# A fused attention and gated-MLP kernel on one core: the written order of its pieces and their engines, written anew

## The chip, the cores and the metric

The kernel runs on one core of a Trainium2 chip. The metric is the device time of one execution in microseconds, the median of several. A core has five engines with instruction streams of their own: TensorE (PE in the profile, with its weight loads as PEld), VectorE (DVE), ScalarE (ACT), GpSimd (POOL) and SyncE (SP), which here issues nearly all DMAs. Each executes its stream in order and waits on semaphores for the others.

## The reference

```python
def _attn_ref(q, k, v):                      # (8, 8, 576, 64) each
    factor, Sd = 4, S // 4
    scale = 1.0 / np.sqrt(D)
    q_d, k_d, v_d = (mean over groups of 4 positions of q, k, v)
    out_d = softmax(scale * q_d @ k_d.T) @ v_d          # 144 x 144, whole
    out_up = np.repeat(out_d, factor, axis=2)
    mask = np.abs(pos[:, None] - pos[None, :]) < factor  # a band of 7
    out_local = softmax(where(mask, scale * q @ k.T, -1e9)) @ v
    return out_up + out_local

def _moe_ref(x, w_in, g_ln, w_sg, b_sg, w_out):          # x: (8, 576, 512)
    h = gelu_tanh(x @ w_in)                              # 1024 wide
    u, v = h[..., :512], h[..., 512:]
    v_n = (v - mean(v)) / np.sqrt(var(v) + 1e-06) * g_ln
    v_s = np.einsum('ts,bsd->btd', w_sg, v_n) + b_sg[None, :, None]
    return x + (u * v_s) @ w_out
```

The attention's output, with its heads side by side, is the `x` of the second function.

## The kernel before

The work is cut into 2105 named pieces (`Task`), each a few instructions of one engine. The program does not run them in loops: a string, `ORDER`, lists all pieces, and the program emits them in that order, so each engine's stream is the string with the other engines' pieces taken out. A word is a name, and after a slash the engine where there is a choice (V VectorE, A ScalarE, P GpSimd, S the SP queue). `place` also reads the string: it gives every piece that takes a buffer the one that was freed longest ago, out of 8 PSUM banks (`ps`), 10 buffers of kind `X` and 38 of kind `R` (`SIZES`). So the order also sets which earlier reader a piece has to wait for.

There are 8 batches, each with 4 pairs of heads, hence 32 pairs `g`. Names of a pair carry `g`; names of the second part carry the batch and an index.

- Loads on SP: `lq`, `lk`, `lv`, `lw` (q, k and two forms of v; 293, 293, 448 and 320 KB), `w…` (weights, 512 KB each; `wq0` to `wq4`, 288 KB), `small` (constants and the band mask, 463 KB) and `b`.
- Weights: `wq`, `wu`, `wb`, `wt`, `wh`, `wl` turn each weight into a high and a low part, once, on ScalarE, VectorE and Pool.
- Attention of a pair: `qs`, `ks`, `vs` sum groups of four. TensorE makes scores, `S` (local, line 424) and `Y` (pooled, line 445) for the first four pairs and both in one piece `YS` afterwards. Then come mask (`ma`, `mb`, line 432), maxima (`mx`, `my`), biases (`nx`, `ny`, lines 461 to 475), exponentials on ScalarE (`ea`, `eb`, line 484; `ec`, line 492), sums (`re`, `rc`), normalisation (`np`, `nq`, lines 506 and 509), transposes on TensorE (`T`, `U`, `t`, lines 512 and 521), their copies out of PSUM (`pa`, `pb`, `pc`, `pe`, line 221), and the product with v on TensorE (`D`, lines 573 and 589). `oe`, `od`, `xa`, `xb` join both results to `x` (line 596), `xh` and `xl` split it in a high and a low part (lines 221, 608), `xc` copies a rest.
- Second part of a batch: on TensorE `v` (line 691; in batch 0 split by its inner index into `vk` pieces and `v0.…`), `u` and `s` and `o` (all line 769; 12, 14 and 12 matmuls of 288 columns; in the last batch four `o` are split into `ok` and a rest). Between them `vg`, `vb`, `vp`, `vn`, `vh`, `vl` (activation, statistics, root, normalisation at line 740, split), `ua` (gelu, line 788), `sa` (line 807), `sm` (the gate, line 814), `gh`, `gl` (split, line 826), `oa` (line 843) and the store `os` (line 848).

TensorE's matmuls fall in three families: the big pieces `v`, `u`, `s`, `o` on the whole array; `S`, `Y`, `YS` and `D` on quarters of it (64 rows by 64 columns, 48 by 64); and the transposes. The batches overlap freely: attention pieces of the next batch stand between big pieces of this one.

Of the kernel before, what the change touches and what calls it, by code (L numbers as in the profile page):

```python
# [103 lines left out]
vp0.4 vn0.3 ua0.6 ua0.4 whq4/A xb4 vh0.2/A vl0.2/V vn0.4 U5 pa5/A pb5/A ua0.2 ua0.3 u0.5 vl0.1/V vh0.3/A vh0.4/A xh4/A
u0.7 vl0.3/V wur2 whr3/A wlr3/P t5 vl0.4/V wlq4/V s0.0 sa0.0 vs5 sm0.0/V s0.2 lq7 sa0.2 s0.1 eb6 wbr2 pc5/A pe5/A
xl4/V ea6 sa0.1 ua0.1 whr1/A s0.4 re6/V rc6 np6/V s0.3 s0.6 lw5 wtr2 whr0/A sm0.2/P sa0.4 lk8 whr2/A sm0.1/P gh0.0/A
sa0.3 sm0.3/V sm0.4/P qs7/V sa0.6 qs8/V ks8/V gl0.0/V s0.5 nq6/P lw6 ua0.5 gh0.1/A gl0.1/P ua0.7 sa0.5 sm0.5/V xc4
s0.7 sm0.6/P T6 D5 YS7 lq9 lv6 gh0.2/A sa0.7 sm0.7/V gl0.2/V wlr1/P my7 pa6/A lw7 oe5/V od5 ma7 gh0.3/A mb7 mx7 U6 xa5
gl0.3/P o0.6 vs6 oa0.6 lk9 wlr0/V xb5 ny7/A ec7 t6 pb6/A pc6/A pe6/A nx7/A ea7 o0.7 qs9/V D6 oe6/V od6 lv7 oa0.7 os0.3
vs7 YS8 lk10 lq10 wlr2/P eb7 ma8 mb8 mx8 nx8/V ea8 my8 re7/V xa6 rc7 np7/V o0.4 oa0.4 o0.5 oa0.5 ny8/A o0.1 nq7/P T7  # L110
U7 xh5/V eb8 xl5/V xc5 ec8 t7 ks9/V o0.3 pa7/V pb7/V pc7/V o0.0 pe7/V D7 re8/V rc8 xb6 oa0.0 oa0.1 oe7/V lv8 od7 xa7
YS9 lq11 ma9 lk11 nq8/P np8/P T8 U8 xh6/A xl6/P xb7 my9 xh7/A mb9 mx9 ny9/A t8 ec9 pa8/A pb8/V pc8/A xl7/P pe8/V xc7
nx9/A v1.1 vg1.1 vb1.1 vs8 v1.0 vg1.0 qs10/V lw8 D8 lv9 xc6 ks10/V oe8/V od8 ks11/P v1.4 va1.4/V ea9 eb9 re9/A vb1.0
v1.3 xa8 vg1.3 vj1.4 vg1.4 vp1.1 vn1.1 rc9 np9/V v1.2 vg1.2 T9 vs9 nq9/V U9 xb8 vp1.0 vn1.0 vh1.0/A pa9/A vl1.0/P
vb1.3 vh1.1/V pb9/A YS10 my10 ny10/A lq12 ma10 mb10 ec10 mx10 lw9 nx10/A pc9/A t9 pe9/V o0.2 oa0.2 vb1.2 u1.4 D9 oa0.3
qs11/P YS11 vp1.3 vb1.4 lk13 eb10 vn1.3 vh1.3/V lw11 os0.0 ea10 vp1.2 vn1.2 vp1.4 ma11 mb11 lv10 mx11 my11 ny11/V u1.2
re10/A rc10 oe9/A od9 xa9 u1.3 lq13 vl1.3/P vh1.2/A vl1.2/P u1.0 ua1.0 u1.1 np10/P T10 vn1.4 vh1.4/V ua1.4 nq10/P t10
ua1.2 vl1.4/P ua1.1 vs10 U10 pa10/A pb10/A vl1.1/V s1.1 pc10/V sa1.1 s1.0 ec11 nx11/A pe10/A xb9 lw10 D10 eb11 oe10/A
lk12 ks12/V qs12/V sa1.0 ks13/V lv11 YS12 my12 ma12 s1.2 ea11 re11/A rc11 sm1.1/P nq11/V ny12/A ec12 mb12 s1.4 vs11
mx12 nx12/V eb12 ea12 od10 ua1.3 s1.3 re12/A u1.6 lk14 os0.2 qs13/V xa10 xb10 sm1.0/V sa1.2 sm1.2/P gh1.0/A u1.5 xh9/V  # L120
lq14 np11/V U11 ua1.6 sa1.3 sm1.3/V t11 T11 pa11/A gh1.1/V s1.5 rc12 nq12/V pb11/V xh8/A pc11/A qs14/P t12 xl9/V
np12/V sa1.5 sa1.4 pe11/A D11 YS13 ua1.5 oe11/A od11 xa11 xb11 lv12 vs12 T12 ma13 lk15 mb13 mx13 nx13/A eb13 u1.7
xh10/V s1.6 my13 sm1.4/V gl1.0/P ua1.7 xl8/V xc9 ny13/V sm1.5/V ea13 pa12/A ec13 re13/A s1.7 xh11/V xl11/P xl10/V v2.3
vg2.3 v2.0 vg2.0 sa1.6 sm1.6/P sa1.7 sm1.7/V gh1.2/V gl1.2/P v2.1 gh1.3/V gl1.3/P gl1.1/P o1.4 vg2.1 U12 pb12/A rc13
np13/V T13 oa1.4 nq13/P U13 pc12/A pe12/A xc11 lw12 ks14/V D12 YS14 lv13 lq15 qs15/V vb2.1 xc8 pa13/A pb13/A pc13/V
vs13 my14 ma14 mb14 ny14/A ec14 t13 pe13/V oe12/V od12 xc10 v2.4 va2.4/A ks15/P o1.5 mx14 u2.6 nx14/V ea14 eb14 o1.2
vp2.1 vn2.1 oa1.5 ua2.6 o1.0 vb2.0 vp2.0 vj2.4 vn2.0 vh2.0/V vl2.0/V vb2.3 xa12 xb12 oa1.0 lw13 lq16 qs16/V D13 YS15
ma15 lv14 oa1.2 my15 mb15 o1.6 oa1.6 vg2.4 vb2.4 oe13/V vs14 mx15 od13 vh2.1/A nx15/V lw15 o1.7 re14/V rc14 xa13 lk16
ks16/P v2.2 ny15/A vp2.4 vn2.4 o1.1 ec15 vg2.2 vb2.2 oa1.1 os1.0 u2.0 np14/P T14 pa14/A nq14/V t14 vp2.3 U14 vl2.1/V
pb14/A o1.3 vh2.4/A vp2.2 vn2.2 pc14/A vh2.2/V lw14 ua2.0 pe14/V xb13 eb15 vn2.3 vh2.3/V D14 lv15 oa1.7 YS16 ma16  # L130
oa1.3 vl2.2/V u2.4 ea15 mb16 u2.3 my16 ny16/V ec16 oe14/A vl2.4/P u2.5 xh13/V lq18 lq17 re15/A rc15 xh12/V od14 qs17/V
u2.1 vs15 xa14 mx16 nx16/V ua2.4 ua2.5 np15/V nq15/V vl2.3/P s2.1 eb16 s2.0 sa2.0 xb14 u2.2 xh14/V xl14/V sa2.1 ua2.1
u2.7 ea16 re16/A ua2.2 ua2.3 lw16 lk17 xl12/V qs18/V sm2.1/V rc16 np16/V sm2.0/V s2.2 gh2.0/A s2.3 sa2.3 U15 T16 t15
# [855 lines left out]
```

## Time and profile before

| what | value |
|---|---|
| timed executions | 586.85, 587.50, 587.54 us; median 587.5 |
| profiled execution, span from first to last instruction | 585.7 us |
| TensorE busy | 559.7 us, 96% |
| VectorE, ScalarE, Pool busy | 432.7, 354.0, 306.2 us |
| DMA | 63.21 MB, mean 108 GB/s |

The timed median lies 1.8 us above the profiled span. Busy time of TensorE counts modelled ends of pipelined matmuls, so a full row does not say that it could not be faster; the distance between the starts of two pieces is the better measure of what a piece costs.

### The profile page before, as it was taken

Reading aid. Unit: us, or ns where it says so; the run is one execution under the profiler, and the core shown is the slowest. Engines: PE = TensorE matmul, PEld = TensorE weight load, DVE = VectorE, ACT = ScalarE, POOL = GpSimd, SP = SyncE. Lnnn points to the kernel's source line nnn. Section 1 sums busy time; section 2 is a strip of 40 time slices with the busy share of each in tenths; the row PEclk is TensorE's granted clock in tenths of the full one; section 3 lists DMA queues with packets and bytes.
Section 4 is the critical chain, followed back from the end, with each engine's and each line's share of the span. In section 5 each row is a group of like instructions: output and inputs, shape, how many; then the busy total and the mean of one; then the engine's idle time right before and its main releaser. Section 6 shows DMA issues by size and latency. Waiting matters only on the chain.

```text
span 585.7 us, 17441 instructions
## 1 busy us (share of the span) xinstructions
PE 559.7 (96%) x6992; PEld 522.2 (89%) x6992; DVE 432.7 (74%) x947; ACT 354.0 (60%) x1227; POOL 306.2 (52%) x384
## 2 busy tenths in 40 slices
PE   4778999999999999999999999999999999999997
...
GB/s 318 305 281 286 14 48 128 158 118 137 144 26 98 97 83 58 96 157 63 16 134 193 13 194 90 59 134 42 37 62 230 118 100 1 113 1 1 41 2 121
DMA packets 30610, 63.21 MB, mean 108 GB/s; under 512 B 3520, under 2 KB 3776, under 8 KB 30528
## 3 DMA queue, kind: packets, MB, share of 16 engines
...
q10 hardware_dynamic: 576, 1.23, 0.6%
...
## 4 chain that ended last, share of the span: by engine, by line
PE 81%; DVE 8%; ACT 5%; issue 3%; DMA 1%; POOL 0%; SPq 0%; ACTq 0%; DVEq 0%; POOLq 0%
PE ps L769 49%; PE ps L691 15%; PE ps L573 4%; ACT X L484 3%; PE ps L512 3%; PE ps L589 3%; PE ps L424 2%; PE ps L445 2%; PE ps L521 2%; DMA small_sb<-in_small_dram 1%; ACT pd L492 1%; DVE R L740 1%; DVE wsg_l L352 1%; DVE st L721 1%; ACT L492 1%
## 5 line engine op out<-in xcount | busy, mean ns | idle before, releaser
L769 PE MATMUL ps<-wsg_h,R 128*128 128x288 f32 x576 | 120.8, 297 | 0.0
L769 PE MATMUL ps<-R,weight_r 128*128 128x288 f32 x768 | 109.4, 297 | 0.3 <-ACT pd L492 0.3
L769 PE MATMUL ps<-X,weight_z 128*128 128x288 f32 x512 | 108.2, 296 | 0.3 <-DVE X L432 0.3
L769 PEld LDWEIGHTS ps<-R,weight_r 128*128 128x128 f32 x768 | 103.8, 188 | 2.1 <-DVE R L826 0.4
L691 PE MATMUL ps<-weight_y,X 128*128 128x512 f32 x320 | 98.0, 400 | 0.1
L484 ACT ACTIVATE X<-X,nb 128x64 f32<-128x64 f32 x280 | 93.5, 338 | 3.2 <-DVE nb L463 2.8
L769 PEld LDWEIGHTS ps<-wsg_h,R 128*128 128x128 f32 x576 | 94.2, 188 | 0.2
L769 PE MATMUL ps<-wsg_l,R 128*128 128x288 f32 x320 | 92.8, 296 | 0.4 <-DVE wsg_l L352 0.4
L769 PEld LDWEIGHTS ps<-X,weight_z 128*128 128x128 f32 x512 | 83.9, 188 | 1.2 <-ACT weight_z L221 0.7
L769 PE MATMUL ps<-R,weight_z 128*128 128x288 f32 x256 | 75.4, 295 | 0.0
L691 PEld LDWEIGHTS ps<-weight_y,X 128*128 128x128 f32 x320 | 58.2, 189 | 12.5 <-POOL X L221 0.4
L769 PEld LDWEIGHTS ps<-wsg_l,R 128*128 128x128 f32 x320 | 60.2, 188 | 0.6 <-DVE wsg_l L352 0.6
L732 POOL TENSOR_TENSOR rs<-rs,nhalf 128x1 f32<-128x1 f32 (+1 forms) x40 | 24.5, 614 | 63.0 <-DVE rs L723 62.9
L807 DVE SCALAR_TENSOR_TENSOR vs<-ps,small_sb,b_sb 128x288 f32<-128x288 f32 x64 | 32.4, 513 | 32.6 <-PE ps L769 31.6
L484 ACT ACTIVATION_READ_ACCUMULATOR X<-X,nb 128x1 f32 x280 | 53.1, 190 | 0.0
L691 PE MATMUL ps<-weight_y,R 128*128 128x512 f32 x128 | 50.7, 396 | 0.0
L408 POOL TENSOR_TENSOR pairs<-R 112x256 f32<-112x256 f32 x56 | 44.6, 796 | 10.2 <-DMA R<-in_v_dram 10.2
L788 ACT ACTIVATE R<-ps 128x288 f32<-128x288 f32 x64 | 24.7, 411 | 40.9 <-PE ps L769 40.8
L221 ACT CAST R<-R 128x512 fp32r<-128x512 f32 (+2 forms) x44 | 28.0, 641 | 34.0 <-DVE R L814 14.2
L769 PEld LDWEIGHTS ps<-R,weight_z 128*128 128x128 f32 x256 | 48.1, 188 | 0.3
L826 POOL TENSOR_TENSOR R<-R,R 128x576 fp32r<-128x576 f32 x21 | 31.1, 1484 | 28.6 <-PE ps L521 14.4
L814 POOL TENSOR_TENSOR R<-R,vs 128x288 f32<-128x288 f32 x23 | 20.4, 894 | 45.2 <-DVE vs L807 39.2
(111 smaller groups left out, 1210.7 us busy)
## 6 DMA issues: line engine op xcount, KB each, us to landing
...
```

Of the source, the lines that this page charges most:

```text
L221: (nc.scalar.copy if e == "A" else ENG[e].tensor_copy)(**kw)
L408: ENG[e].tensor_tensor(out=pairs, in0=v[:, 0:2], in1=v[:, 2:4], op=ALU.add)
L484: nc.scalar.activation(out=st["ms"][:, t, :], in_=src, func=AF.Exp, bias=st["nb"][:, t:t + 1], scale=scale, accum_out=sums[par][:, t:t + 1])
L512: nc.tensor.matmul(out=out, lhsT=st["ms"][0:LD, 2 * c:2 * c + 2, :], rhs=turn_l, is_transpose=True, start=True, stop=True)
L573: nc.tensor.matmul(out=out, lhsT=lhsT, rhs=pdt[ks, probs, h * QC:(h + 1) * QC], start=first, stop=last)
L691: nc.tensor.matmul(out=acc, lhsT=r32(l), rhs=r32(weights[f"y{k}"][:, 0, w]), start=(i == 0 and ks[0] == 0), stop=(i == len(ops) - 1 and ks ...
L732: nc.gpsimd.tensor_tensor(out=rs[0:n], in0=rs[0:n], in1=nhalf[0:n], op=ALU.pow)
L769: nc.tensor.matmul(out=acc[:, 0:HALF], lhsT=r32(l), rhs=r32(r), start=(first and n == 0), stop=(last and n == len(ops) - 1))
L788: nc.scalar.activation(out=us[i // 2][:, half(i)], in_=at["ps", "m", b, "u", i][:, 0:HALF], func=AF.Gelu_apprx_tanh)
L807: nc.vector.scalar_tensor_tensor(out=vsb[i], in0=at["ps", "m", b, "s", i][:, 0:HALF], scalar=g_sb[:, i // 2:i // 2 + 1], in1=b_sb[:, half( ...
L814: ENG[e].tensor_tensor(out=u[:, half(i)], in0=u[:, half(i)], in1=vsb[i], op=ALU.mult)
L826: ENG[e].tensor_tensor(out=r32(gl[d]), in0=us[d], in1=gh[d], op=ALU.subtract)
```

## The change

The string `ORDER` is replaced by another order of the same 2105 pieces, with other choices of engine for some. No function, buffer count or instruction shape changes. The new string was sought by a planner with rules in which VectorE and Pool exclude each other and TensorE pays for changes between kinds of pieces; the planner is not part of the kernel. Of the choices, the gate `sm` is on Pool 30 times instead of 23 (of 64), `np` and `nq` 39 instead of 34 (of 64), `vh` on VectorE 20 instead of 15 (of 40). Both strings up to `v0.1`, and their ends:

```diff
-wy0 lk0/A lq0/A lq1/A small ks0/P wqy0/A wuy0 wby0 wty0 wy3 qs0/V S0 mx0 lw1/A qs1/P nx0/V ea0 why0/V wqy3/V Y0 my0
-lk1/S ks1/P wy1 wuy3 wby3 wqy1/V ny0/A ec0 wly0/P wby1 wty3 wuy1 wty1 wy2 wqy2/A S1 wuy2 wby2 Y1 my1 wty2 lq3 wz2 eb0
-mx1 re0/A rc0 ny1/A ec1 nx1/A ea1 nq0/P lk3 np0/P lk2 wuz2 S3 lq2 S2 wz3 wqz2/V wbz2 mx3 qs3/V lq4 mx2 eb1 wqz3/A T0
-pa0/V why3/V U0 t0 pb0/A lv0/S lw0/S nx2/A pc0/V pe0/V ks2/P qs2/P Y2 my2 re1/A rc1 ks3/P ny2/V D0 ea2 eb2 wbz3 qs4/V
-wz1 np1/P oe0/V ec2 re2/A nq1/P lk4 ks4/P lv1/S wtz2 od0 xa0 xb0 T1 pa1/A t1 U1 pb1/V pc1/V pe1/A nx3/A Y3 my3 ea3 rc2
-np2/P nq2/P wqz1/A ny3/A YS4 xh0/V ma4 mb4 my4 mx4 eb3 ec3 wz0 D1 xl0/P lv2 wbz1 nx4/V T2 lw2 lq5 U2 re3/V oe1/A
-wly3/P rc3 np3/P lk5 whz2/A wlz2/P t2 pa2/A wqz0/A pb2/V pc2/V wq3 vk3.0 pe2/A qs5/V ny4/A ec4 D2 wr0 od1 xa1 wuz0
-nq3/P wbz0 eb4 T3 vk1.0 lv4 lv3 oe2/V od2 ks5/P xa2 xb2 xb1 lw3 pa3/A wq1 lk6 t3 U3 pb3/V pc3/V wr3 xh1/V why1/A
-wly1/V YS5 pe3/A D3 ma5 my5 ea4 re4/A rc4 nq4/V wuz3 lw4 t4 oe3/V wtz0 xl1/P vk3.1 why2/A wly2/P mb5 wr1 xh2/A xl2/V
-ks6/V ny5/A mx5 ec5 b lq6 od3 xa3 xb3 xh3/V np4/P xc0 wqr0/A lv5 wur0 wtz3 vk0.0 vk0.1 wq2 xc2 wqr1/A xl3/V nx5/A
-qs6/V vk0.2 vk2.0 vk2.1 wbr0 vk2.2 vk4.0 wqr3/A wur3 ea5 eb5 vs4 wbr1 wuz1 vk1.1 vk1.2 v0.1 lk7 re5/A wtr0 T4 pa4/A
...
-vh7.3/A vl7.3/V vl7.2/P oa6.1 os6.0 ua7.3 s7.0 s7.1 sa7.1 sa7.0 sm7.0/V ua7.5 sm7.1/P s7.2 sa7.2 sm7.2/P s7.4 sa7.4
-sm7.4/P ua7.6 ua7.7 s7.3 sa7.3 s7.5 gh7.0/V sm7.3/V gh7.1/V sa7.5 sm7.5/V gl7.1/P gh7.2/V s7.7 s7.6 o6.6 gl7.2/P
-gl7.0/V ok0 ok2 sa7.7 sm7.7/V ok1 sa7.6 sm7.6/P gh7.3/V gl7.3/P o7.0 oa7.0 o7.4 oa7.4 o7.5 oa7.5 oa6.6 o7.1 oa7.1 o7.2
-oa7.2 ok3 oa6.7 os7.2 os6.3 o7.6 oa7.6 os7.0 o7.3 os6.2 oa7.3 os7.1 o7.7 os7.3.0 oa7.7 os7.3.1
+lq0/A lk0/S ks0/V qs0/P Y0 my0 ny0/A small ec0 wy3 wuy3 wqy3/V wby3 wty3 wy1 wuy1 wqy1/V lq1/S qs1/P S0 mx0 lk1/S
+ks1/V nx0/A ea0 eb0 wby1 S1 mx1 Y1 my1 nx1/V re0/A ea1 lq2 why3/V ny1/V ec1 lk2 qs2/P S2 lw0/S ks2/P rc0 np0/V T0 wq0
+nq0/P U0 lq4 mx2 nx2/A wly3/V pa0/V pb0/V pc0/V lv0/S t0 eb1 pe0/A whq0/V wty1 why1/V wly1/P lk3 ks3/V lq3 S3 re1/A
+ea2 Y2 qs4/P wy2 lk4 rc1 D0 my2 ny2/A ec2 np1/P wy0 mx3 nx3/A wqy0/A oe0/V od0 xa0 xb0 wqy2/V xh0/V xl0/P T1 pa1/V wz2
+qs3/V ks4/P wby0 wq3 whq3/V wuy0 eb2 re2/A rc2 wby2 YS4 ma4 nq1/P U1 pb1/V wz1 wqz1/A xc0 wz3 wqz2/A ea3 mb4 my4 Y3
+my3 ny4/V wuy2 eb3 wq4 lq5 qs5/V pc1/V mx4 lv1/S lk5 ny3/A t1 pe1/A wlq0/P np2/P T2 pa2/A ec3 re3/A wbz2 wuz3 rc3 wbz1
+nq2/P U2 wty0 t2 wty2 pb2/A wuz1 wuz2 pc2/A pe2/V ks5/V ec4 lw1/S D1 oe1/V np3/P YS5 T3 od1 xa1 wqz3/A why0/A nx4/V
+xb1 wly0/V vk3.0 wtz2 nq3/P U3 xh1/V xl1/P lv2 whq4/A lw2 wtz1 ea4 pa3/A vk2.0 ma5 eb4 lv3 my5 ny5/A re4/A mb5 wbz3
+lk6 ks6/P pb3/A pc3/A wlq4/V rc4 np4/P D2 oe2/V od2 xa2 wr1 wqr1/A vk0.0 t3 lq6 ec5 wr2 why2/A wqr2/A wtz3 pe3/A mx5
+nx5/A lw6 xb2 xh2/A vk3.1 whz1/A vk2.1 vk0.1 wbr1 lw3 whz2/A wz0 wqz0/A wuz0 wr0 vk4.0 T4 pa4/V xc1 wly2/P vk1.0 wbr2
+vk4.1 vk1.1 D3 xl2/P xc2 vk4.2 vk2.2 vk1.2 whz3/A wbz0 oe3/A nq4/P U4 eb5 ea5 vk0.2 od3 xa3 xb3 vk3.2 wlz3/V wq1
+whq1/A xh3/V t4 wtz0 lk12 xl3/V xc3 v0.1 pb4/A wlq3/V lq7 wlz1/V qs7/V qs6/V wlz2/P vg0.1 vb0.1 lv4 vs4 re5/V v0.2
...
+u7.7 o6.2 oa6.2 vl7.0/V u7.1 u7.6 vl7.2/V vp7.3 vn7.3 vh7.3/V ua7.6 ua7.7 ua7.0 ua7.1 u7.2 u7.4 ua7.4 ua7.2 vn7.4
+vl7.3/V vh7.4/V vl7.4/V s7.1 sa7.1 s7.5 sm7.1/V s7.0 s7.2 s7.3 sa7.0 sm7.0/P sa7.2 gh7.0/V ua7.3 sa7.3 sm7.3/V sa7.5
+ua7.5 sm7.2/P gh7.1/A s7.4 sa7.4 sm7.4/P gl7.1/V gl7.0/P sm7.5/V gh7.2/V o6.5 s7.6 s7.7 gl7.2/V ok3 ok2 ok1 sa7.7
+sm7.7/P oa6.3 os6.1 ok0 sa7.6 oa6.5 sm7.6/P gh7.3/V gl7.3/V o7.4 o7.5 os3.0 o7.1 oa7.4 oa7.5 os6.2 o7.3 os5.0 os6.0
+o7.0 oa7.0 os7.2 oa7.1 os7.0 o7.2 oa7.2 oa7.3 os7.1 o7.6 oa7.6 os7.3.0 o7.7 oa7.7 os7.3.1
```

More of the change, by code (lines that the diff above doesn't have):

```diff
@@ L104 @@
[L104 to L133, printed above, removed]
@@ L144 @@
-os1.3 sa3.0 sm3.1/V sm3.0/P gh3.0/A xl17/P re18/A rc18 np18/V lq21 qs21/V s3.2 s3.3 ua3.4 u3.5 ua3.5 ua3.3 s3.4 s3.5
-oa2.5 sa3.2 sm3.2/V np19/P lw19 sa3.4 sm3.4/V sa3.3 sm3.3/V nq18/P gl3.0/P gh3.1/V U19 sa3.5 lw18 t18 T18 pa18/A xc16
-ua3.7 xc17 gl3.1/P U18 pb18/A sm3.5/V gh3.2/A pc18/V T19 pa19/A pb19/V pc19/V s3.6 s3.7 sa3.6 pe19/V pe18/A D18 lv19
-vs19 sa3.7 sm3.7/V YS20 ma20 mb20 oe18/A od18 xa18 D19 gl3.2/P sm3.6/P gh3.3/A oe19/A gl3.3/P o3.7 my20 lv20 xb18
-ny20/V ec20 o3.4 mx20 xh18/V lq22 od19 xa19 xb19 xh19/V nx20/A eb20 YS21 my21 ma21 lk23 mb21 mx21 oa3.4 nx21/V lq23
@@ L184 @@
-sm6.4/P ua6.5 sm6.5/V s6.7 gl6.1/V s6.6 sa6.6 sa6.7 sm6.7/V D30 lv31 vs31 pe31/A gh6.2/A gl6.2/V os4.0 oe30/A D31
-sm6.6/P gh6.3/A gl6.3/V o6.3 od30 xa30 o6.0 o6.1 xc28 xb30 xh30/V oe31/V o6.2 oa6.2 o6.5 o6.4 od31 xa31 xb31 xl30/P
-xh31/V xl31/V xc31 oa6.4 xc29 xc30 v7.4 oa6.0 va7.4/V u7.6 u7.2 ua7.2 vj7.4 v7.1 u7.0 ua7.0 v7.2 vg7.1 vb7.1 vp7.1
-vg7.2 vb7.2 vp7.2 v7.0 vg7.0 vb7.0 v7.3 vg7.3 vn7.1 vh7.1/V vn7.2 vp7.0 vn7.0 vb7.3 vg7.4 u7.7 vb7.4 vh7.0/A vl7.1/P
-oa6.3 vl7.0/P u7.1 o6.7 vh7.2/A vp7.4 vn7.4 vh7.4/A ua7.1 os5.1 oa6.5 u7.3 vl7.4/V vp7.3 u7.4 ua7.4 vn7.3 os6.1 u7.5
```

136 lines of the change are left out of this document (87 added, 49 removed).

## The prediction

> **What bounds the kernel now.** I read the page first, then busy time by windows, the waits of TensorE, its timeline at the front and around some changes of kind, the chain of work, the loads' issues, and the groups of VectorE.
>
> ```profile
> span 585.7 us, 17441 instructions
> PE 559.7 (96%) x6992; PEld 522.2 (89%) x6992; DVE 432.7 (74%) x947; ACT 354.0 (60%) x1227; POOL 306.2 (52%) x384
> ...
> PE   4778999999999999999999999999999999999997
> ```
>
> TensorE is busy 96% of the span, and its idle share sits in the first fifth. The next view has columns of length, then busy microseconds of each engine, granted clock, DMA share and GB/s.
>
> ```profile
> 0.00:64.00 64.00, 45.70 (x847) 36.87 (x848) 43.10 (x98) 43.23 (x198) 40.36 (x52) 0.89 0.86 275
> 64.00:124.00 60.00, 58.82 (x810) 55.88 (x809) 55.33 (x117) 47.42 (x145) 44.28 (x46) 1.00 0.32 100
> 124.00:544.00 420.00, 417.38 (x5054) 391.90 (x5053) 312.53 (x695) 258.66 (x876) 209.27 (x275) 1.00 0.29 89
> 544.00:586.00 42.00, 37.82 (x286) 37.59 (x284) 21.78 (x41) 4.74 (x11) 12.29 (x12) 1.00 0.16 58
> ```
>
> So there are four stages: a front of 64 us in which DMA (0.86) is the fullest resource; 60 us in which VectorE (55.33 of 60) runs as full as TensorE; 420 us of TensorE alone; and a tail. The waits of TensorE after the front are these:
>
> ```profile
> PE ps L445 <- DVE vs L807: 0.8, 1, 0.8
> PE ps L424 <- issue: 0.5, 1, 0.5
> PE ps L512 <- DVE X L506: 0.5, 1, 0.5
> PE ps L445 <- DVE R L596: 0.5, 1, 0.5
> PE ps L445 <- DVE X L432: 0.4, 1, 0.4
> PE ps L769 <- DVE wsg_l L352: 0.4, 1, 0.4
> PE ps L769 <- DVE X L432: 0.3, 1, 0.3
> PE ps L769 <- ACT pd L492: 0.3, 1, 0.3
> ```
>
> They sum to 3.7 us. I matched every TensorE instruction with its piece in the written order and took each piece's usual start-to-start time from undisturbed places. At these prices the order needs 547.0 us of TensorE from the first start to the start of o7.7, which comes at 580.1. So TensorE is 33.1 us late there, and 5.6 us follow. The lateness is 25.0 us at v0.1, 27.1 at v1.1 and 33.1 at the end: some 8 us of stalls after the front, about twice what the wait rows show, because a wait is counted only from the modelled end of the matmul before and short ones are not listed.
>
> **The change, part by part.** No instruction is added or removed except table loads of ScalarE, which follow the order (60 changes of function become 56, and ScalarE has room). What can change is what TensorE pays between kinds, and where it waits.
>
> *Changes between kinds.* Starts are the first column:
>
> ```profile
> 543.16 38.68 PE ps L769 x292
> ...
> 306.62 0.58 PE L512 MATMUL ps<-small_sb,X 122*128 122x122 f32 x4
> 306.96 0.51 PE L769 MATMUL ps<-wsg_h,R 128*128 128x288 f32 x2
> ...
> 308.91 0.42 PE L769 MATMUL ps<-wsg_h,R 128*128 128x288 f32 x2
> ...
> 310.85 0.64 PE L573 MATMUL ps<-R,vd 48*64 48x144 f32 x15
> ...
> 311.84 0.29 PE L445 MATMUL ps<-kd,qd 64*64 64x144 f32 x1
> ...
> 312.84 0.28 PE L573 MATMUL ps<-R,vd 48*64 48x144 f32 x1
> ...
> 314.01 1.07 PE L769 MATMUL ps<-R,weight_r 128*128 128x288 f32 x6
> ```
>
> The first row gives 0.1325 us a matmul in a long run, so 1.86 for an s piece of 14. Here s3.6 starts at 306.96 behind a transpose and takes 1.95 (+0.09), s3.7 takes 1.94 because D18 follows (+0.09). D18 (310.85) takes 0.99 with YS20 behind it, D19 takes 1.17 with a big piece behind it (+0.17), and that big piece pays about 0.1 more. One excursion into D and YS pieces thus costs 0.09 + 0.17 + 0.10 = 0.36 us. Counted in the orders, TensorE enters D and YS pieces from elsewhere 32 times before and 35 after: +1.1 us. Transposes leave for a big piece 35 times before and 83 after, but inside a run a T takes 0.42, and at its end 0.34 plus 0.09 on the next piece: about 0.01 each, +0.5 us. The new order therefore costs TensorE **+1.6 us**: by the count, changes between kinds do not become fewer or cheaper.
>
> *The front.* Rows of TensorE, of the clock windows, and of the issue of the last early load:
>
> ```profile
> 8.54 2.50 PE L417 MATMUL ps<-small_sb 128*128 128x256 f32 x4 [8.54 <-DMA small_sb<-in_small_dram]
> ...
> 26.62 3.25 PE L573 MATMUL ps<-R,R 48*64 48x144 f32 x58
> ...
> 40.41 0.60 PE L573 MATMUL ps<-R,R 48*64 48x48 f32 x11 [3.11 <-issue]
> ...
> 45.77 1.97 PE L573 MATMUL ps<-R,R 48*64 48x144 f32 x60
> ...
> 48.41 0.64 PE L512 MATMUL ps<-small_sb,X 122*128 122x122 f32 x4
> ...
> 54.34 1.38 PE L573 MATMUL ps<-R,R 48*64 48x144 f32 x49 [2.05 <-issue]
> ...
> 56.48 0.40 PE L521 MATMUL ps<-small_sb,pd 112*112 112x112 f32 x2
> ...
> 63.54 0.63 PE L691 MATMUL ps<-weight_y,X 128*128 128x512 f32 x2
> ```
> ```profile
> 26.00:33.00 7.00, 6.91 (x122) 6.48 (x119) 5.05 (x13) 5.14 (x32) 5.18 (x7) 0.52 0.78 204
> 33.00:39.50 6.50, 3.92 (x123) 3.17 (x121) 5.96 (x15) 5.16 (x30) 4.64 (x4) 1.00 1.02 326
> 39.50:46.40 6.90, 5.99 (x81) 5.13 (x84) 2.69 (x9) 3.66 (x13) 4.62 (x6) 0.51 1.05 334
> ```
> ```profile
> 37.09 0.35 SPq L386 DMA_DIRECT2D X<-in_vw_dram  x1
> ```
>
> The first matmul waits 8.54 us for the small constants, behind 1.9 MB in written order; the new order has 1.07 MB up to there, so at some 300 KB/us S0 comes 2 us earlier. D0 (26.62) has 19.1 us of VectorE, 17.4 of ScalarE and 16.0 of Pool pieces ahead of it; in the new order 15.9, 13.3 and 11.0, so it can start near 22. Against that, D3 has 47.9 us of VectorE ahead instead of 37.5, and lw3 stands at 13.75 MB instead of 12.7: issued at 37.09 it landed near 43, so at the same rate near 46.6. What moves ahead of D3 is work that must be done anyway: 10 of the 15 vk pieces instead of 2. From D3's end (56.48) to v0.1 (63.54) TensorE now works 7 us; in the new order 4.1. Walking VectorE's new order by hand with the rows' durations gives it 47.7 us of work up to xl3, 4.6 us of waiting for the first load and about 8 us of gaps: v0.1 near 61.0, with 41.6 us of TensorE work behind it against 38.5, so lateness 19.4 instead of 25.0. That is an undisturbed walk. D2 (45.77 to 48.41) takes an undisturbed 2.64 us; D0 took 2.1 more at half clock, D1 4.6 more and D3 2.1 more with the "issue" stalls of the rows. No order removes their cause, and I charge 3.6 us for their like. The front gives **−2.0 us**.
>
> *The stretch that VectorE shares.* From xl3 to v1.1 the old order has 60.3 us of VectorE work for 58.0 of TensorE, the new one 59.9 for 57.0: 0.6 more surplus, **+0.5 us**. VectorE's own price is uncertain here:
>
> ```profile
> L814 DVE TENSOR_TENSOR R<-R,vs x41: 445/460/1358, 89.3 to 567.4; 128x288 f32<-128x288 f32 x41
> ```
> ```profile
> L463 DVE TENSOR_SCALAR nb<-stats x16: 156/173/1108, 13.1 to 488.9; 128x10 f32<-128x10 f32 x16
> L814 DVE TENSOR_TENSOR R<-R,vs 128x288 f32<-128x288 f32 x41 | 27.1, 664 | 3.8 <-ACT R L788 2.2
> ```
>
> The same gate multiplication takes 445 to 1358 ns (min, median, max), and a 10-element scaling up to 1108: the long ones lie beside Pool instructions. Over all groups such excess is about 32 us of the 432.7. I take no change in it, because it is Pool work that must run some time.
>
> *The stalls after v1.1* are 6.0 us. Where a piece stands with less than 1 us of TensorE work between it and the place of what it needs, it is exposed. Counted, T, U, t and D stand so 50 times in 111 before and 14 times in 109 after; pieces that take a PSUM bank whose last reader is so close, 85 in 470 against 20 in 468. From a YS to its transposes lies a median of 16.1 us of other work before, 24.3 after. I let 3.5 of the 6.0 us go; the bounds are 0 and 6. The gain's cover is that other engines do keep their place, which is the first rival.
>
> *The tail.* The last s pieces are followed by four ok pieces (4.8 us) that cover sa, sm, gh and gl of the last block (about 4.2) in both orders, and the same o7.6, o7.7 and half stores end it.
>
> ```profile
> 576.79 5.89 SPq L848 DMA_DIRECT2D out_dram<-R  x7
> ```
>
> Seven stores are issued at the end before; in the new order os3.0 and os5.0, ready long before, stand among them, which makes ten. SP waits there for oa6.3 and oa6.5 with these behind it, but no load is left to wait. Their 0.6 MB is hidden by the o7 pieces if DMA moves 300 KB/us as in the front; with that cover gone it costs up to 2 us. I take 0.
>
> **Sum.** 585.7 + 1.6 − 2.0 + 0.5 − 3.5 = 582.3 us of span. The timed executions' median, 587.5, is 1.8 above the profiled span, so **584.1 us**, 0.6% faster.
>
> **Rivals.** *VectorE stays the bound (slower).* Up to TensorE's own time of 138 us (s1), the old order has 92.7 us of VectorE work for 99.5 of TensorE from v0.1, so VectorE gets free; the new one has 96.1 for 96.4. If VectorE can be busy no more than in the shared stretch (55.33 of 60, 0.92), 96.1 takes 104.2 us: 7.8 late, where the old order lost 2.1 in the whole stretch to v1.1. It replaces my +0.5 by +5.7: 589.3. It decides once VectorE's gaps pass 5% there. For it: such sums stay near zero in the new order up to 150 us. Against: the leads above are long, so a late VectorE has some 8 us to give. Chance 0.18.
>
> *The waits only move (same).* The front's gain is eaten by the half clock and new waits of like size follow: 585.7 + 1.6 − 1.5 + 0.5 − 1 + 1.8 = 587.1. The clock is the mechanism: each half-clock stretch in the rows lasts some 6.9 us, and a third one over full work costs half of it, 3.4 us. In the new order D1 is followed by a wait for YS5 of about 3 us, a place for it. Chance 0.20. [...]
>
> *VectorE and Pool really step aside (faster still).* If the new order keeps Pool out of the way, the long cases go: L814 alone spends 27.1 us where 41 × 0.46 would be 18.9, so 8.2 us. In the shared stretch, where VectorE counts, the excess over all groups is some 5 us: 579.1. It is against this that in the 420 us stage VectorE is not the bound at all. Chance 0.12. [...]
>
> **How the numbers follow.** My sum holds 0.50, its own range 580 to 587. What this kernel's measurement can tell from no change is about 0.2%, so 586.3 to 588.7 is the same. Faster: 0.45 of my case, 0.12 of the third rival and 0.05 of the second: 0.62. Same: 0.05 + 0.13, and 0.01 of the first: 0.19. Slower: 0.17 + 0.02: 0.19. The range that leaves out 2 in 10 reaches from below the third rival to above the first: with the store bound on top, 577 to 591.
>
> **What would show it.** S0 before 7 us and D0 near 22 show the loads right; v0.1 later than 64 shows the front wrong. VectorE above 0.92 of the window from 64 to 160 with waits of TensorE on L807, L740 or L596 shows the first rival. The waits of TensorE after 128 us should sum to under 2 us. Clock below 1 after 60 us, or a store landing later than 4 us after the last o_add, would break the sum.

## The result, and the profile after

The new order takes 582.98 us (median of 9 runs, 580.98 to 584.36); the kernel before took 587.5 (9 runs) beside it on the same chip. The ratio is 0.9931, with a 95% interval of 0.9904 to 0.9958: 0.7% faster, where the prediction said 584.1 us and 0.6%. The profiled execution's span fell from 585.7 to 580.5 us.

The page of the new order, its first lines, columns as before:

```profile
span 580.5 us, 17400 instructions
...
PE 555.8 (96%) x6992; PEld 518.5 (89%) x6992; DVE 423.9 (73%) x926; ACT 350.5 (60%) x1237; POOL 312.1 (54%) x388
...
PE   5679999999999999999999999999998999999997
```

TensorE executes the same 6992 matmuls and is busy 3.9 us less (559.7 before), and its row fills earlier: the first four slices read 5679 where they read 4778. Busy time that falls at equal work points to fewer microseconds at half clock, and the windows show where (length, busy time of each engine, granted clock, DMA share, GB/s):

```profile
0.00:64.00 64.00, 48.28 (x895) 39.00 (x898) 51.82 (x116) 49.12 (x212) 43.88 (x55) 0.97 0.94 309
64.00:124.00 60.00, 57.96 (x852) 55.14 (x846) 55.23 (x111) 44.48 (x162) 45.86 (x53) 1.00 0.43 130
124.00:544.00 420.00, 416.43 (x5005) 391.43 (x5006) 299.52 (x669) 253.58 (x856) 216.18 (x276) 1.00 0.25 78
544.00:586.00 42.00, 33.13 (x251) 32.90 (x249) 17.30 (x33) 3.31 (x9) 6.17 (x6) 0.98 0.17 64
...
27.60:31.00 3.40, 3.25 (x64) 2.83 (x68) 2.34 (x7) 2.99 (x18) 3.40 (x5) 0.50 1.02 241
```

What has changed for TensorE and the clock is the front of 64 us (the tail is shorter because the program ends earlier): VectorE does 51.8 us of work there instead of 43.1, the granted clock is 0.97 instead of 0.89, DMA 0.94 instead of 0.86. One stretch of 3.4 us at half clock is left in the front (last row), where the old order had two, together 13.7 us by the trace's clock records (25.9 to 32.7 and 39.5 to 46.4). The second and third stage hold about as much TensorE time as before.

These are two single executions, and the one of the new order has the highest clock of its nine: 0.997 over the whole span, the others 0.988 to 0.994, the median 0.991. In 62 executions of the old order that were timed beside the experiments the median is 0.988. Over a span those medians come to some 10 us at half clock in a typical execution of the new order against 14 in the old, by my estimate. Time and clock go together in the old order: its executions at 0.994 or more took 581.6 to 584.5 us, those at 0.985 or less 586.9 to 589.9. The new order took 581.0 to 582.3 at 0.994 or more and 584.3 at 0.988. So part of the gain of 4.5 us goes with half clock that comes less often, and at equal clock less than 4.5 is left; the shares are not settled.

In TensorE's timeline (start, busy time, instruction, and in brackets the idle time before it) the front reads:

```profile
7.33 2.50 PE L417 MATMUL ps<-small_sb 128*128 128x256 f32 x4
...
20.24 1.62 PE L573 MATMUL ps<-R,R 48*64 48x144 f32 x58
...
27.75 0.88 PE L445 MATMUL ps<-kd,qd 64*64 64x144 f32 x10 [3.57 <-POOL kd L395]
...
34.79 1.74 PE L573 MATMUL ps<-R,R 48*64 48x144 f32 x58 [0.62 <-ACT pd L492]
...
51.60 1.71 PE L573 MATMUL ps<-R,R 48*64 48x144 f32 x60
...
58.66 0.70 PE L691 MATMUL ps<-weight_y,X 128*128 128x512 f32 x2
```

S0 starts at 7.33, D0 at 20.1 (its first two matmuls stand in a row just ahead of the one shown), YS4 at 27.75 behind a wait of 3.57 us for Pool, D1 at 34.79, D3 at 51.60, v0.1 at 58.66 instead of 63.54. The waits of TensorE (sum, times, longest) are now:

```profile
PE ps L445 <- POOL qd L395: 6.1, 1, 6.1
PE ps L445 <- POOL kd L395: 3.6, 1, 3.6
PE ps L589 <- issue: 2.2, 1, 2.2
PE ps L445 <- DVE kd L391: 1.9, 1, 1.9
...
PE ps L769 <- DVE R L760: 0.7, 1, 0.7
PE ps L769 <- DVE R L826: 0.6, 1, 0.6
...
PE ps L445 <- ACT R L788: 0.6, 1, 0.6
```

The first one starts the program (Y0 comes first now); the second and fourth are in the front (YS4 and YS5). The 2.2 us for "issue" stand at 442.6 us, in the middle of D27.

I use the prediction's measure throughout: lateness, that is the start of a piece less all TensorE work ahead of it at the usual start-to-start prices. Spans and lateness are those of one profiled execution each. All runs:

| kernel | timed median, us | ratio to before, 95% interval | span | lateness at v0.1 | at v1.1 | at o7.7 |
|---|---|---|---|---|---|---|
| before | 587.5 | 1 | 585.7 | 25.1 | 27.1 | 33.1 |
| new order | 582.98 | 0.9931 [0.9904, 0.9958] | 580.5 | 17.1 | 20.3 | 26.7 |
| e1 new to v0.1, then old | 582.47 | 0.9928 [0.9902, 0.9954] | 580.4 | 17.1 | 20.8 | 27.2 |
| e2 old to v0.1, then new | 596.43 | 1.0161 [1.0124, 1.0199] | 595.6 | 24.2 | 33.7 | 42.4 |
| e3 new order, old engines | 659.2 | 1.1255 [1.1215, 1.1295] | 657.5 | 40.0 | 51.8 | 103.6 |
| e4 old order, new engines | 671.65 | 1.1449 [1.1405, 1.1493] | 670.5 | 30.1 | 44.4 | 118.4 |
| e5 vk back behind D3 | 584.51 | 0.9965 [0.9938, 0.9992] | 583.4 | 20.3 | 23.6 | 29.6 |
| e6 before, YS4 behind D1 | 588.19 | 1.0023 [0.999, 1.0056] | 588.4 | 27.8 | 29.4 | 35.7 |
| e7 new, YS29 ahead of s5.7 | 580.95 | 0.9896 [0.9851, 0.9942] | 578.3 | 16.3 | 19.1 | 24.1 |
| e8 new, ks4 ahead of xl0 | 582.73 | 0.9942 [0.9913, 0.9971] | 581.1 | 18.1 | 21.3 | 27.2 |
| e9 new to D0, then old | 601.5 | 1.0245 [1.0217, 1.0273] | 600.8 | 40.6 | 42.4 | 48.6 |
| e11 front written again | 595.05 | 1.0136 [1.0113, 1.016] | 596.2 | 22.3 | 36.0 | 41.4 |
| e12 the same, second writing | 604.27 | 1.0291 [1.0266, 1.0316] | 604.2 | 24.9 | 43.4 | 50.0 |
| e13 e7 and two more moves | 582.55 | 0.9923 [0.9905, 0.9941] | 581.2 | 17.2 | 21.5 | 26.9 |

### The profile page after: what moved, and what is told of

Its sections match the earlier page's. It is cut to its first block, busy times and chain, and to the rows that moved or that the text cites. A ratio compares the mean times of both kernels' runs of the same rounds, so it can differ in the third digit from the quotient of the medians.

```text
span 580.5 us, 17400 instructions
## 1 busy us (share of the span) xinstructions
PE 555.8 (96%) x6992; PEld 518.5 (89%) x6992; DVE 423.9 (73%) x926; ACT 350.5 (60%) x1237; POOL 312.1 (54%) x388
## 4 chain that ended last, share of the span: by engine, by line
PE 82%; DVE 9%; POOL 3%; issue 3%; ACT 2%; DMA 1%; DVEq 0%; ACTq 0%; POOLq 0%
PE ps L769 50%; PE ps L691 17%; PE ps L445 3%; PE ps L512 2%; PE ps L521 2%; PE ps L424 2%; PE ps L589 2%; PE ps L573 2%; POOL R L826 1%; POOL R L814 1%; DMA R<-in_qT_dram 1%; DVE R L221 1%; DVE R L596 1%; DVE X L432 1%; DVE R L740 1%
## 5 line engine op out<-in xcount | busy, mean ns | idle before, releaser
L769 PE MATMUL ps<-wsg_h,R 128*128 128x288 f32 x576 | 122.9, 300 | 1.2 <-DVE R L760 0.7
L769 PE MATMUL ps<-X,weight_z 128*128 128x288 f32 x512 | 110.9, 299 | 0.0
L691 PE MATMUL ps<-weight_y,X 128*128 128x512 f32 x320 | 99.2, 402 | 0.3 <-DVE weight_y L326 0.2
L732 POOL TENSOR_TENSOR rs<-rs,nhalf 128x1 f32<-128x1 f32 (+1 forms) x40 | 23.3, 587 | 82.6 <-DVE rs L723 76.7
L814 POOL TENSOR_TENSOR R<-R,vs 128x288 f32<-128x288 f32 x30 | 27.8, 929 | 44.5 <-DVE vs L807 43.3
L221 ACT COPY R<-ps 112x288 f32<-112x288 f32 (+4 forms) x75 | 27.8, 391 | 38.6 <-PE ps L521 16.2
L408 POOL TENSOR_TENSOR pairs<-R 112x256 f32<-112x256 f32 x56 | 46.7, 834 | 3.6 <-DMA R<-in_v_dram 3.5
L721 DVE BATCH_NORM_STATS2 st<-R 128x6 f32<-128x512 f32 (+1 forms) x40 | 27.4, 686 | 27.5 <-ACT R L703 25.8
```

The lines of the kernel that those rows point to most:

```text
L221: (nc.scalar.copy if e == "A" else ENG[e].tensor_copy)(**kw)
L408: ENG[e].tensor_tensor(out=pairs, in0=v[:, 0:2], in1=v[:, 2:4], op=ALU.add)
L691: nc.tensor.matmul(out=acc, lhsT=r32(l), rhs=r32(weights[f"y{k}"][:, 0, w]), start=(i == 0 and ks[0] == 0), stop=(i == len(ops) - 1 and ks ...
L721: nc.vector.bn_stats(out=st6[0:n], in_=v[0:n])
L732: nc.gpsimd.tensor_tensor(out=rs[0:n], in0=rs[0:n], in1=nhalf[0:n], op=ALU.pow)
L769: nc.tensor.matmul(out=acc[:, 0:HALF], lhsT=r32(l), rhs=r32(r), start=(first and n == 0), stop=(last and n == len(ops) - 1))
```

## The experiments

**e1 and e2: which part of the string carries the gain.** The strings are cut at v0.1 and joined crosswise; pieces that the first half has not yet are taken in the other string's sequence, with that string's engines (some lines at the seam, - the new order, + e1; then - the old order, + e2).

```diff
-v0.1 pb4/A wlq3/V lq7 wlz1/V qs7/V qs6/V wlz2/P vg0.1 vb0.1 lv4 vs4 re5/V v0.2
+v0.1 wlz2/P lv4 wr3 lw4 b wqr0/A lv5 wur0 wq2 qs6/V wbr0 wqr3/A wur3 vs4 lk7 re5/A wtr0 rc5 np5/V
...
-vk1.1 vk1.2 v0.1 lk7 re5/A wtr0 T4 pa4/A
+vk1.1 vk1.2 v0.1 wq0 whq0/V whq3/V wq4 wlq0/P whq4/A wtz1 wlq4/V wr2 wqr2/A lw6 whz1/A T4 pa4/V
```

> The new order up to v0.1, then the remaining pieces in the old sequence. Front theory (all the gain is made before v0.1 and is kept): lateness at v0.1 near 17 us instead of 25, span near 578.5, 1.2% below the kernel before, even a little below the new order. Rival, the gain is given back where VectorE is shared: lateness at v0.1 near 17, but at v1.1 near 25 to 27 again, span 584 to 586. Rival, the gain is made all along the order: lateness at v1.1 and span no better than before, 586 or more.

> The mirror image: the old order up to v0.1, then the remaining pieces in the new sequence. Front theory: lateness at v0.1 near 25 us, at the last piece near 34, span 586 to 588.5, no faster than the kernel before. Rival, the later parts carry the gain: 583 or less of span. My prediction's own split (front -2.0, stalls after v1.1 -3.5) would give some 583.9.

e1 is as fast as the whole new order (its span of 580.4 us lies between the front theory's 578.5 and the first rival's 584). Lateness is 17.1 at v0.1 as expected; 3.6 us are lost right behind the seam (2.1 at D4, where this row of e1's waits stands, and 1.2 behind YS6), and from s0.0 to the end the old sequence adds 6.5 against 8.7 in the new order.

```profile
PE ps L573 <- POOL R L319: 2.1, 1, 2.1
```

So the front is enough for all of the gain, and the later part of the new order adds none. e2 has the old lateness at v0.1 (24.2) and ends even later than expected: 4.8 us go at vk4.1, which waits for a small Pool copy that the new sequence has ahead of v0.1 and e2 only behind the seam.

```profile
PE ps L691 <- POOL X L221: 4.6, 1, 4.6
```

Its other 3 us up to s0.0 I can't assign one by one. A cut string has a seam that costs some microseconds by itself, so e2 shows that the later part doesn't bring the gain, and not that it is 9 us worse.

**e3 and e4: places or engines.** Of the 718 pieces with a choice 328 change their engine. e3 is the new sequence with each piece on its old engine, e4 the old one with the new engines, throughout; at the beginning:

```diff
-lq0/A lk0/S ks0/V qs0/P Y0 my0 ny0/A small ec0 wy3 wuy3 wqy3/V
+lq0/A lk0/A ks0/P qs0/V Y0 my0 ny0/A small ec0 wy3 wuy3 wqy3/V
```

> The new order of the pieces, every piece on the engine it had before. Theory that the places of pieces and loads carry the change: lateness at v0.1 17 to 20 us, span 579 to 583. Rival, order and engines only work together: with the old engines VectorE has 8.8 us more to do (432.7 against 423.9 busy), pieces of the front come late, lateness at v0.1 above 22 and span above 585.

> The old order of the pieces, with the new choices of engine. Theory that places carry the change: lateness at v0.1 near 25 us, span 585 to 588. Rival, the engines carry it (fewer collisions of VectorE with Pool): span below 583 and less than 28 us of excess over the short durations on VectorE (32.6 before, 32.5 after by the same count).

Both theories fell: each half of the change alone costs 72 to 85 us. Here are the same 420 us of e3, then of e4:

```profile
124.00:544.00 420.00, 384.53 (x4630) 354.30 (x4629) 293.00 (x639) 239.32 (x820) 204.18 (x261) 0.97 0.27 83
```
```profile
124.00:544.00 420.00, 378.46 (x4658) 347.89 (x4652) 274.48 (x610) 238.45 (x841) 193.00 (x252) 0.96 0.29 88
```

No engine is full: TensorE fell to 385 and 378 of 420, VectorE to 293 and 274. The lateness grows everywhere, in dozens of steps of 0.3 to 9 us, whose waits end on VectorE, ScalarE, Pool and loads. With no engine full, the amount of work does not explain it; the reading that is left, which no run tests alone, is the place of the work: a piece put into a stream that wasn't written for it makes what stands behind it in that stream late, as one late load does with ScalarE's work in e9 (17.5 us). So neither "places" nor "engines" can be credited alone. The excess of VectorE over its short durations was 42.8 us in e3 and 32.6 in e4 (32.6 before, 32.5 after): the new engines don't bring that excess down.

**e5: the vk pieces ahead of D3.** Eight of ten go back behind it:

```diff
-vk0.0 ... vk3.1 ... vk2.1 vk0.1 ... vk4.0 T4 pa4/V xc1 wly2/P vk1.0 wbr2 vk4.1 vk1.1 D3 xl2/P
+T4 pa4/V xc1 wly2/P vk1.0 wbr2 D3 vk2.0 vk0.0 vk3.1 vk2.1 vk0.1 vk4.0 vk4.1 vk1.1 xl2/P
```

> The new order with eight of the ten vk pieces that stand ahead of D3 put back behind it. Theory that the front gains because TensorE has vk work at hand while the attention pieces wait: lateness at v0.1 rises from 17 toward 22 us and the span by 3 to 5.6 us, to 583.5 to 586. Rival, the front's gain is only that two stalls at half clock and for "issue" did not come (D1 4.6 and D3 2.1 before): lateness at v0.1 stays within 1 us of 17 and the span near 580.5.

Lateness at v0.1 rises by 3.2 us and the span by 2.9: the first theory, just below its numbers. (The intervals of the two ratios overlap, so this rests on the traces.) The timeline of e5 shows T4 now waiting with nothing to do, and the matmuls behind it at half clock (0.63 where 0.39 is usual), and the windows the clock (in the trace's clock record the half clock lasts 3.4 us, from 48.1 to 51.5):

```profile
47.66 0.68 PE L512 MATMUL ps<-small_sb,X 122*128 122x122 f32 x4 [2.16 <-POOL X L506]
48.05 1.15 PE L691 MATMUL ps<-weight_y,X 128*128 128x512 f32 x2
49.01 0.63 PE L691 MATMUL ps<-weight_y,R 128*128 128x512 f32 x1
```
```profile
49.00:53.00 4.00, 4.00 (x107) 3.38 (x106) 3.37 (x6) 2.63 (x6) 3.94 (x6) 0.68 1.04 256
```

**e6 and e7: the stalls for "issue".** In both orders the longest of them (3.11 us in the old one, 2.21 in the new) stand in a run of short instructions of TensorE (a matmul and its weight load each): Y3, YS4 and D1 in the old order, YS29, D26 and D27 in the new one. The page has the instructions on DMA queues of their own; the larger one:

```profile
q8 instruction: 55, 0.90, 0.6%
```

55 packets of 16 KB (16384 bytes each in the trace), and 13984 matmuls and weight loads: one packet for some 254 if all were for TensorE, an estimate. e6 edits the old order, e7 the new one:

```diff
-np2/P nq2/P wqz1/A ny3/A YS4 xh0/V ma4 mb4 my4 mx4 eb3 ec3 wz0 D1 xl0/P
+np2/P nq2/P wqz1/A ny3/A xh0/V eb3 ec3 wz0 D1 YS4 ma4 mb4 my4 mx4 xl0/P
...
-gh5.2/A s5.7 sa5.7 sm5.7/V YS29 ma29 my29
+gh5.2/A YS29 s5.7 sa5.7 sm5.7/V ma29 my29
```

> The old order with YS4 behind D1, so that Y3, YS4 and D1 (352 short instructions of TensorE, matmuls and weight loads) no longer follow each other. Theory that the 3.11 us "issue" stall is TensorE running through its short instructions faster than they are brought in: the stall inside D1 goes, D1 takes 2.6 to 3.2 us instead of 7.2, and the span falls by up to 4, as far as the later YS4 does not cost it again. Rival, the stall belongs to the place in the stream or in time (near 38 us): it stays 2 us or more, and the span is 586 or more.

> The new order with YS29 ahead of s5.7, so that YS29, D26 and D27 (336 short instructions) no longer follow each other. Theory that a long run of short instructions is what stalls for "issue": the 2.2 us of that wait at 441.6 us go, at the price of one more entry into short pieces (0.36), span 578 to 579. Rival, the stall belongs to the place of a 16 KB fetch in the stream: a stall of about 2 us stays at o5.6 or near it, span 580.5 to 581.

e6 was drawn wrongly: behind Y3 there are D1 and YS4 now instead of YS4 and D1, so the run is as long as it was, only in another order. What it gave is of use all the same. The stall stays, and moves from the middle of D1 to the border of D1 and YS4 (e6's timeline):

```profile
35.14 0.80 PE L589 MATMUL ps<-R,X 64*64 64x58 f32 x34
40.60 0.83 PE L445 MATMUL ps<-kd,qd 64*64 64x144 f32 x11 [4.67 <-issue]
```

The trace's records of these packets, each set beside the count of matmuls and weight loads issued:

| kernel | TensorE stands after | next packet starts, takes | TensorE goes on |
|---|---|---|---|
| before | 937 | 38.0, 0.9 | 40.41 |
| e2 | 937 | 37.7, 1.3 | 40.53 |
| e6 | 937 | 37.8, 1.4 | 40.60 |
| new order | 11570 | 442.2, 1.2 | 444.83 |
| e8 | 11570 | 443.1, 1.0 | 445.39 |

TensorE stands at the same count, also where other pieces make it up (e6), and goes on 1.3 to 1.6 us after the packet's end. In these five it had issued 339 to 449 instructions since the packet before. So in these five traces the place goes with the count in the stream, not with the pieces. That a stall comes where TensorE has used up what was brought before the next packet is there is my reading: the records do not say which instructions a packet holds. In e7 s5.7 lies in the run, the packet starts with 264 issued, at 438.0, and TensorE runs through (e7's timeline):

```profile
441.24 0.81 PE L589 MATMUL ps<-R,X 64*64 64x58 f32 x38
441.98 3.47 PE L769 MATMUL ps<-R,weight_r 128*128 128x288 f32 x24
```

The 2.46 us of D27 are gone, at 0.36 for one more entry; 0.84 came back at v6.1, which now has to wait for VectorE's split. The span is 2.2 us shorter, of which 0.8 arose ahead of v0.1, where nothing was changed. The interval of e7 overlaps that of the new order, and e13 holds the same move without a shorter time; that the stall goes is shown, that the kernel gets faster by it is not.

**e8: the longest wait of the new front.** Pool's ks4 stands ahead of xl0 instead of behind:

```diff
-xh0/V xl0/P T1 pa1/V wz2 qs3/V ks4/P wby0
+xh0/V ks4/P xl0/P T1 pa1/V wz2 qs3/V wby0
```

> The new order with ks4 ahead of xl0 in Pool's stream. TensorE's longest wait of the new front, for ks4 ahead of YS4, gets shorter by some 3 us, as ks4 can start at 23.5 instead of 26.5. Theory that Pool's queue bounds the front: lateness at v0.1 falls from 17.1 to about 14, span 577.5. Rival, VectorE's pieces behind it (pa1, pb1, my4, pc1) bound the front: YS4 comes 2 to 3 us earlier, D1 hardly, lateness at v0.1 16.5 to 17.2, span 580 to 580.5.

The rival held in kind; lateness at v0.1 (18.1) and span (581.1) came out a little above its numbers. The waits of e8 in its timeline:

```profile
25.95 1.03 PE L445 MATMUL ps<-kd,qd 64*64 64x144 f32 x4 [1.79 <-DVE R L221]
27.93 0.82 PE L445 MATMUL ps<-kd,qd 64*64 64x144 f32 x12 [0.95 <-DVE R L311]
...
35.15 2.16 PE L573 MATMUL ps<-R,R 48*64 48x144 f32 x31 [0.95 <-ACT sums L497]
```

YS4 starts 1.8 us earlier, then TensorE waits for VectorE, and D1 comes at 35.15 instead of 34.79. The wait named Pool; the waits that follow it are for VectorE and ScalarE.

**e9: the start alone.** The new order up to D0, then the old one:

```diff
-Y2 qs4/P wy2 lk4 rc1 D0 my2 ny2/A ec2 np1/P wy0 mx3 nx3/A wqy0/A oe0/V od0 xa0 xb0
+Y2 qs4/P wy2 lk4 rc1 D0 wy0 wqy0/A wuy0 wby0 wty0 lw1/A why0/V wly0/P wqy2/A wuy2 wby2 wty2
```

> The new order up to D0, then the remaining pieces in the old sequence. Theory that the early start is the gain (loads in smaller portions, S0 and D0 sooner): D0 near 20 at a lateness of 7 instead of 13.4, and the 6 us last to v0.1, lateness there 18 to 20. Rival, the start is given back because the other engines are no further: lateness at D1 16 to 18 and at v0.1 22 to 26, span 583 or more, as the new order's own lateness grew from 6.9 at D0 to 14.6 at D1.

Inconclusive. D0 stood at 20.0, lateness 6.8, but then ScalarE waited 17.5 us: the load lw1, which the old order issues from ScalarE's queue, was issued at 40.6 only, with all of ScalarE's work behind it (waits of ScalarE).

```profile
ACT weight_y L303 <- DMA R<-in_v_dram: 17.5, 1, 17.5
```

The trace's semaphore records say what lw1 waited for. In the traces of both orders the 220 DMA issues use eight semaphores, 27 or 28 each, and none of the 212 with an earlier one on its semaphore starts before that one has landed. In e9 lw1 stands on semaphore 100; the load before it there is one of v that SP issued at 33.2, whose last part landed at 40.54, and lw1 goes out at 40.56. So the cut string gave lw1 a late turn among the semaphores (why so late is not shown), and e9 says nothing about the early start. That the early start is mostly given back is read from the new order's own trace (below), not from e9.

**e11 and e12: a denser front.** Both are e7 with everything up to v1.1 put in another order, sought with the durations of these traces, attention pieces ahead of weights. They differ in some hundred places; of e11:

```diff
-D0 my2 ny2/A ec2 np1/P wy0 mx3 nx3/A wqy0/A oe0/V od0 xa0 xb0 wqy2/V xh0/V xl0/P T1 pa1/V wz2 qs3/V ks4/P wby0 wq3 whq3/V wuy0
+D0 eb2 oe0/V ec2 od0 xa0 T1 pa1/A wz2 ks3/P re2/V xb0 U1 rc2 lw1/S qs4/P pb1/V ea3 pc1/A wby2 Y3 t1 YS4
```

> The new order with YS29 ahead of s5.7, and all up to v1.1 written once more: attention pieces of pairs 1 to 3 ahead of weight pieces on VectorE, ScalarE and Pool (wby0, wby2, wuy0, whq3 and the like later), 78 engine choices changed. Theory that the front is bound by VectorE's and ScalarE's order behind D0: D1 near 30 instead of 35, v0.1 near 50 to 53 at a lateness of 10 to 13, span 571 to 575. Rival, a front this dense runs into stalls for "issue" and half clock: lateness at v0.1 15 or more, span 577 or more.

> A second writing of the same front by the same rule, with 73 other engine choices. Expected as for the first: v0.1 near 50 to 53 us, span 571 to 576; by the rival 577 or more. If the two differ by more than 3 us at v0.1 while their pieces are the same, the difference shows what such stalls cost.

The rival held, and more: v0.1 came at 61 to 63 us, and lateness grew by another 13.7 and 18.5 us up to v1.1. The first two windows of e11, then of e12:

```profile
0.00:64.00 64.00, 45.47 (x847) 36.04 (x847) 53.27 (x103) 42.58 (x195) 43.79 (x55) 0.89 0.95 306
64.00:124.00 60.00, 55.84 (x742) 51.72 (x743) 54.80 (x104) 44.46 (x147) 46.28 (x51) 0.91 0.32 96
```
```profile
0.00:64.00 64.00, 47.84 (x845) 37.57 (x845) 49.27 (x102) 42.38 (x184) 41.53 (x51) 0.84 0.89 284
64.00:124.00 60.00, 53.95 (x670) 49.50 (x671) 51.57 (x101) 44.42 (x138) 44.63 (x53) 0.89 0.38 118
```

The clock is below 1 in the second stage too, which no row of either original shows, and TensorE is busy 566.6 and 571.8 us for work that took 555.8. A reading that fits, but that no run tests: an order laid out from undisturbed durations leaves no room behind each wait; one that comes a little late idles TensorE, and the half clock after it makes the rest late. Which of the many moves began it stays open. (Both profiled executions are the slowest of their six; the others took 594.7 to 595.2 and 602.0 to 604.6 us.)

**e13: two more waits taken away.** To e7:

```diff
-u0.3 ua0.3 vl0.0/V ... YS7 ... D4 oe4/V qs9/V vl0.4/V my7 s0.1
+vl0.0/V ... YS7 ... D4 oe4/V qs9/V vl0.4/V my7 u0.3 ua0.3 s0.1
...
-o5.0 oa5.0 vl6.4/P vl6.3/P s6.0 ... s6.5 o5.1
+o5.0 oa5.0 vl6.4/P vl6.3/P o5.1 s6.0 ... s6.5
```

> The new order with YS29 ahead of s5.7, and two big pieces moved: u0.3 (with ua0.3) from ahead of YS7 to behind D4, o5.1 ahead of s6.0. Theory that a wait behind the front goes when other work of TensorE is put ahead of the exposed piece: the 0.93 us at s0.1 to s0.0 and the 0.66 at o5.0 to s6.0 (waits on L760) go, the stalls behind v0.1 sum to 6.2 instead of 7.7 and the span falls by 1.5 from 578.3, to about 576.8. Rival, the waits move on to the next piece: the two places are clean, but others grow by as much and the span stays within 0.5 of 578.3.

It missed: the step from s0.1 to s0.0 is now 1.45 instead of 0.93, and the 0.66 went from s6.0 to o5.1, ahead of it. The row of e13's waits names ScalarE's gelu, which u0.3 had moved behind D4 with it:

```profile
PE ps L769 <- ACT R L788: 1.1, 1, 1.1
```

Putting other work ahead of an exposed piece helps only if that work's own readers don't stand in the same place.

## Why the prediction was right, term by term

| term | predicted | found, at the same prices |
|---|---|---|
| changes between kinds | +1.6 | +1.7 |
| front, up to v0.1 | −2.0 | −8.0 |
| stretch from v0.1 to v1.1 | +0.5 | +1.2 |
| stalls after v1.1 | −3.5 | +0.4 |
| tail | 0 | −0.5 |
| span | −3.4 | −5.2 |

The total lies within 1.8 us, but two terms were wrong by 6.0 and 3.9 in opposite directions. The time was right partly by luck.

*Changes between kinds.* Right. The prices taken from a handful of rows give 548.7 us for the new order (547.0 before). This is a sum at the prediction's own prices, but behind the front no piece's start-to-start time in its trace departs from them by over 0.15 us, some 15 waits apart.

*Front: right on the loads and the vk pieces, wrong on the stalls and the size.* S0 before 7 us was off by little (7.33, so 1.2 us earlier than before where 2 was forecast), D0 near 22 came at 20.1, v0.1 near 61.0 undisturbed, and later with the charge, at 58.66. Two steps failed: the walk of VectorE by hand, which gave a lateness of 19.4 at v0.1, and "I charge 3.6 us for their like". Together they make 23.0; measured is 17.1. Lateness, before and after, is 13.4 and 6.9 at D0, 16.3 and 14.6 at D1, 22.5 and 16.8 at D2, 22.9 and 16.5 at D3, 25.1 and 17.1 at v0.1. So of the 6.5 us won at the start, 4.8 are given back by D1: the other engines were no further. Then 4.0 come in D1, where the old order stands 3.11 us for "issue" and slows down afterwards. The rest comes behind D2. So half of the 8.0 comes with a stall of which the prediction said that no order removes its cause, and whose like it charged; that it is this stall is read from the two traces, and no run takes it away alone.

The half-clock rows give busy TensorE time of 12.9 us before and 3.25 after; at half speed up to half of that is lost, 6.5 and 1.6. The new order's front has no wait for "issue" above 0.6 us, and the vk pieces fill what waits there are: with them behind D3 again, e5 gave back 3.2 us by one wait of 2.16 and one more slow stretch.

By this count at most 1.6 of the 17.1 are of the kind that was charged: the charge was 2.0 too large, and the walk 3.9 too slow. The sum of the two is measured, the split is an estimate. e1 and e7 run the same front with 6.8 us at half clock behind YS4 instead of 3.4 and stand at 17.1 and 16.3 at v0.1, no later: TensorE's waits shrink there instead (ahead of D1 and YS5 to 0.33 and 1.60 us in e7, from 0.62 and 1.93). Slow clock ahead of a wait for another engine cost nothing in these two runs, so the half clock explains less of the front's gain than its length suggests.

*The shared stretch.* The window named for the first rival, in the new order:

```profile
64.00:160.00 96.00, 93.33 (x1368) 87.36 (x1363) 87.79 (x189) 75.16 (x254) 61.28 (x75) 1.00 0.37 111
```

VectorE has 87.79 us of work in 96, 0.914, just below the 0.92 of the prediction, and TensorE's waits on L760 and L826 are those of 0.7 and 0.6 us above. The term was 0.7 short; the rival's 5.7 didn't come.

*Stalls after v1.1: wrong.* They are 6.4 us instead of 6.0. "Where a piece stands with less than 1 us of TensorE work between it and the place of what it needs, it is exposed" did not hold as a price: the old order has three to four times as many such places and loses no more. Its tight pieces mostly arrive in time, and the largest single delay behind v1.1 is 1.1 us. TensorE's waits behind 128 us, which were to sum to under 2, hold 2.2 for "issue" alone. 2.5 of the new 6.4 are this stall in D27, which no counting of leads shows; without it (e7: 5.0 from v1.1 to the end) the order would be 1 us better than before, not 3.5. e1 says the same from the other side: with the old sequence behind v1.1 it also adds 6.4.

*Tail.* SP's row at the end of the new order has ten stores, as counted:

```profile
565.38 12.60 SPq L848 DMA_DIRECT2D out_dram<-R  x10
```

They are hidden: the last piece's start to the end of the span takes 5.1 us instead of 5.6.

*The rivals.* "The waits only move" was right about the later part and wrong about the front, and no third half-clock stretch came in the profiled execution, but one instead of two (the median execution has more, as said above). "VectorE and Pool really step aside" is not shown: the gate multiplication on VectorE still takes 643 ns on average (664 before), in 34 instead of 41 instructions, and the excess over all groups is unchanged.

```profile
L814 DVE TENSOR_TENSOR R<-R,vs 128x288 f32<-128x288 f32 x34 | 21.5, 643 | 0.7
```
